# Three inverse channel stages drawn into the drain, the first two FFN parts split by group, and a new preparation plan

## The chip, the cores and the metric

The kernel runs on one core of one Trainium2 chip. The metric is the device time of one execution in microseconds. A kernel's executions agree within about 0.3%, so medians are given, and the figure that decides between two kernels is a ratio with a 95% interval. All times quoted are of fast runs; the mean granted TensorE clock from 46 to 150 us is 1.00 in the trace of every kernel here.

## The reference

A spectral filter with a residual, then an FFN with a squared ReLU and a residual:

```python
def reference(A_x, A_w_r, A_w_i, B_x, B_w1, B_b1, B_w2, B_b2):   # A_x: 1 x 2048 x 512, bf16; B_x is not read
    def A(x):                       # 2-D FFT, times a complex weight, inverse FFT
        X = rfft2(x) * (A_w_r + 1j * A_w_i)
        return irfft2(X, (2048, 512)).astype(bfloat16)
    def B(x):                       # FFN 512 -> 1792 -> 512
        h = relu(x @ B_w1 + B_b1)
        return (h * h) @ B_w2 + B_b2
    h = A_x + A(layernorm(A_x))
    return h + B(layernorm(h))
```

## The kernel before

The FFT is done with matmuls. Its last step, the inverse along the 512 channels, is done for one group of 128 rows at a time, in pieces that are placed among the FFN's matmuls: `s5` to `turn`. `PLAN[k]` says at which slot of chunk k-1 each piece of chunk k stands. A slot is one part of the FFN (14 up parts, then 4 down parts a group).

```python
def s5(g, ahead=False):                       # inverse channel stage of group g
    pe = bank("p5", "po", 2) if ahead else bank("p5", "pp", 3)
    for lt, tb, o in (...):                   # 4 small matmuls into one bank
        nc.tensor.matmul(pe[:, o:o + tb.shape[1]], lhsT=T2[...], rhs=tb, start=True, stop=True)
    def rest():
        nc.scalar.copy(V[...], pe[:])         # ACT takes the bank out
        nc.scalar.copy(H[:, :, 0:129:128], pe[...])
    if ahead: return rest
    rest()

def s5b(g):                                   # DVE: four operations with two SBUF inputs each
    H = V + V ; H = V - V ; R = H + H ; R = H - H
def s6(g):  matmul(py, lhsT=KI, rhs=R)        # PE
def s6a(g): hs[:, g] = py * WSC + xs[:, g]    # DVE, PSUM -> SBUF
# s6b statistics, rstd (ACT sqrt + DVE reciprocal), norm (DVE -> u),
# turn (transposes of u into UT: by PE for chunks 1 and 2, by DMA for chunks 3 and 4)

PLAN = {
    1: dict(s5=(-1, 1, 4), s5b=(-1, 1, 6), s6=(3, 7, 14), s6a=(3, 12, 14),
            s6b=(9, 14, 14), rstd=(15,), norm=(16, 16, 16), turn=(20, 20)),
    2: dict(s5=(1, 1, 3, 12), s5b=(1, 3, 11, 13), s6=(10, 10, 15, 16), s6a=(10, 10, 15, 16),
            s6b=(13, 16, 16, 16), rstd=(17,), norm=(17, 18, 20, 18), turn=(23, 24)),
    3: ..., 4: ...                            # see the diff
}
CHUNKS = ((0, 2), (2, 5), (5, 9), (9, 13), (13, 16))

def up(f):                                    # one up part of chunk c
    ph = bank("ph", "ph", 3)
    for d in range(ND):                       # 4 matmuls, n = 128 columns x groups of the chunk
        nc.tensor.matmul(ph[:, 0:n], lhsT=W1[:, d, bass.ts(f, P)], rhs=UT[:, d, 0:n], ...)
    nc.scalar.activation(rl, ph, ACT.Relu, ...)
    nc.vector.tensor_tensor(act[:, f], rl, rl, ALU.mult)
    # GpSimd's hb = hs + b2, needed by the output addition, tied to a square:
    mine = [a + f // 3] if c and f % 3 == 1 and f // 3 < b - a else range(a, b) if not c and f == NF - 1 else []
    for g in mine: nc.gpsimd.tensor_tensor(hb[:, g], hs[:, g], b2b, ALU.add)

def down(i, f0, f1):                          # po has two banks; ot = po + hb on DVE, then stored
    ...
    nc.vector.tensor_tensor(ot[:], po[:], hb[:, g, :], ALU.add)
    nc.sync.dma_start(ov[:, g, :], ot[:])     # the sync engine's queue, as the DMA transposes

# drain: groups 0 and 1 alone
rest = [s5(2, True), s5(3, True)]             # in the shadow of their LayerNorm
... LayerNorm, rest[0](), transposes of group 0, then of group 1 ...
s5b(2)
for c in range(5): run(c)
```

Of the kernel before, what the change touches and what calls it, by code (L numbers as in the profile page):

```python
# [15 lines left out]
P = 128  # L16
# [18 lines left out]
def kernel(  # L35
# [16 lines left out]
    nc = tc.nc  # L52
# [6 lines left out]
    ND = D // P  # L59
# [9 lines left out]
    W1 = persist.tile([P, ND, F], BF16, name="W1")  # L69
# [50 lines left out]
    def mm_tile(name, dt=FP32):  # L120
        return ps.tile([P, 4096 // mybir.dt.size(dt)], dt, tag="mm", name=name)
# [132 lines left out]
    def warm(o, n):  # L254

        for _ in range(n):
            nc.tensor.matmul(o, lhsT=ones[:, 0:P], rhs=ones[:], start=True, stop=True)  # L257
# [279 lines left out]
    def to_sqrt():  # L537
# [5 lines left out]
                  c=lambda k: butterfly(k, 1), A=lambda k: times_w(k, 0), B=lambda k: times_w(k, 1),  # L543
# [29 lines left out]
    def bank(name, tag, bufs, dt=FP32):  # L573
        return ps.tile([P, 2048 // mybir.dt.size(dt)], dt, tag=tag, name=name, bufs=bufs)

    Rs, Ys = {}, {}

    def s5(g, ahead=False):



        pe = bank("p5", "po", 2) if ahead else bank("p5", "pp", 3)
        for lt, tb, o in ((1, GI[:, 1, 0:129], 0), (3, GI[:, 3, 1:128], 129), (0, GI[:, 0, 0:128], 256),
                          (2, GIa[:, 1024:1152], 384)):
            nc.tensor.matmul(pe[:, o:o + tb.shape[1]], lhsT=T2[:, 2 * (lt % 2) + lt // 2, g].rearrange("p q s -> p (q s)"), rhs=tb,  # L585
                             start=True, stop=True)

        def rest():
            V = ffn.tile([P, 2, 2, 128], BF16, tag="V", bufs=3, name="V")
            H = ffn.tile([P, 2, 256], BF16, tag="H", bufs=3, name="H")  # L590
            nc.scalar.copy(V[:].rearrange("p e h c -> p (e h c)"), pe[:])  # L591
            nc.scalar.copy(H[:, :, 0:129:128], pe[:].rearrange("p (e h c) -> p e h c", e=2, h=2)[:, :, :, 0])
            Rs[g] = V, H

        if ahead:
            return rest
        rest()
# [67 lines left out]
    def transp(c, half):  # L665
# [11 lines left out]
        else:  # L677
# [1 line left out]


    PLAN = {
        1: dict(s5=(-1, 1, 4), s5b=(-1, 1, 6), s6=(3, 7, 14), s6a=(3, 12, 14),
                s6b=(9, 14, 14), rstd=(15,), norm=(16, 16, 16), turn=(20, 20)),
        2: dict(s5=(1, 1, 3, 12), s5b=(1, 3, 11, 13), s6=(10, 10, 15, 16), s6a=(10, 10, 15, 16),
                s6b=(13, 16, 16, 16), rstd=(17,), norm=(17, 18, 20, 18), turn=(23, 24)),
        3: dict(s5=(4, 5, 7, 15), s5b=(4, 8, 14, 15), s6=(10, 11, 18, 18), s6a=(11, 11, 18, 18),
                s6b=(13, 13, 20, 20), rstd=(16, 22), norm=(17, 17, 23, 23), turn=(19, 19, 23, 24)),
        4: dict(s5=(5, 5, 5), s5b=(5, 6, 7), s6=(10, 10, 14), s6a=(10, 15, 15),
                s6b=(14, 15, 17), rstd=(15, 22), norm=(18, 18, 22), turn=(19, 23, 22)),
    }  # L690

    def prep_steps(c):

        a = CHUNKS[c][0]
        n = CHUNKS[c][1] - a
        steps = []
        for kind, piece in (("s5", lambda k: rest[1]() if c == 1 and k == 1 else s5(a + k)), ("s5b", lambda k: s5b(a + k)),
                            ("s6", lambda k: s6(a + k)), ("s6a", lambda k: s6a(a + k)),
                            ("s6b", lambda k: s6b(a + k, on_act(c, a + k))),
                            ("rstd", lambda k: rstd(c, range(a + 2 * k, min(a + 2 * k + 2, a + n)) if c in BY_DMA else range(a, a + n))),  # L700
                            ("norm", lambda k: norm(c, a + k)), ("turn", lambda k: turn(c, k))):
            steps += [(slot, lambda piece=piece, k=k: piece(k)) for k, slot in enumerate(PLAN[c][kind]) if slot >= 0]
        return sorted(steps, key=lambda step: step[0])

    def mlp_slots(c):
        a, b = CHUNKS[c]
        n = P * (b - a)
        UT = UTs[c]
        act = ffn.tile([P, NF, 512], BF16, tag="act", bufs=2, name="act")
        slots = []  # L710

        def up(f):
            ph = bank("ph", "ph", 3)
            for d in range(ND):
                nc.tensor.matmul(ph[:, 0:n], lhsT=W1[:, d, bass.ts(f, P)], rhs=UT[:, d, 0:n],  # L715
                                 start=(d == 0), stop=(d == ND - 1))
            rl = ffn.tile([P, 512], BF16, tag="rl", bufs=6, name="rl")
            nc.scalar.activation(rl[:, 0:n], ph[:, 0:n], ACT.Relu, bias=b1f[:, f:f + 1], scale=1.0)  # L718
            sq = nc.vector.tensor_tensor(act[:, f, 0:n], rl[:, 0:n], rl[:, 0:n], ALU.mult)  # L719
            mine = [a + f // 3] if c and f % 3 == 1 and f // 3 < b - a else range(a, b) if not c and f == NF - 1 else []  # L720
            for g in mine:
                add = nc.gpsimd.tensor_tensor(hb[:, g, :], hs[:, g, :], b2b[:], ALU.add)  # L722
                tc.add_manual_dep(add.ins, sq.ins.name,
                                  mybir.DependencyInfo(mybir.DependencyClass.Sync, mybir.DependencyReason.DATA),
                                  reason="not before this square")

        state = {}

        def last(i):
            g = a + i  # L730
            ot = ffn.tile([P, D], BF16, tag="ot", bufs=3, name="ot")
            for h in range(2):
                po = bank("po", "po", 2)
                sl = slice(256 * h, 256 * h + 256)
                for f in range(NF):
                    nc.tensor.matmul(po[:, 0:256], lhsT=act[:, f, bass.ts(i, P)], rhs=W2[:, f, sl], start=(f == 0),  # L736
                                     stop=(f == NF - 1))
                nc.vector.tensor_tensor(ot[:, sl], po[:, 0:256], hb[:, g, sl], ALU.add)
                nc.sync.dma_start(ov[:, g, sl], ot[:, sl])

        def down(i, f0, f1):
            if c == 4 and i == b - a - 1:
                return last(i) if f0 == 0 else None
            if f0 == 0:
                state[i] = bank("po", "po", 2)
            po = state[i]
            for f in range(f0, f1):
                nc.tensor.matmul(po[:], lhsT=act[:, f, bass.ts(i, P)], rhs=W2[:, f, :], start=(f == 0), stop=(f == NF - 1))  # L748
            if f1 == NF:
                g = a + i  # L750
                ot = ffn.tile([P, D], BF16, tag="ot", bufs=3, name="ot")
                nc.vector.tensor_tensor(ot[:], po[:], hb[:, g, :], ALU.add)  # L752
                nc.sync.dma_start(ov[:, g, :], ot[:])

        for f in range(NF):
            slots.append(lambda f=f: up(f))
        for i in range(b - a):
            for f0, f1 in ((0, 4), (4, 8), (8, 11), (11, NF)):
                slots.append(lambda i=i, f0=f0, f1=f1: down(i, f0, f1))
        return slots  # L760
# [31 lines left out]
    for g in range(2):  # L792
        py = mm_tile("p6")[:, 0:512]
        if g == 0:
            nc.tensor.matmul(py, lhsT=identW[:], rhs=xs[:, 0, :], start=True, stop=False)
        for h in range(2):
            nc.tensor.matmul(py[:, 256 * h:256 * h + 256], lhsT=KI[:], rhs=R2[g][:, 256 * h:256 * h + 256],
                             start=(g == 1), stop=(g == 1 or h == 1))
        if g == 0:
            nc.scalar.activation(hs[:, 0, :], py, ACT.Copy, scale=WSC, accum_out=mv2[:, 0, 0:1])  # L800
        else:
            nc.vector.scalar_tensor_tensor(hs[:, 1, :], py, WSC, xs[:, 1, :], ALU.mult, ALU.add)
    warm(mm_tile("idle")[:, 0:512], 3)
    ps.release()
    ps = ctx.enter_context(tc.tile_pool(name="ps2", bufs=3, space=bass.MemoryType.PSUM))
    rest = [s5(2, True), s5(3, True)]
    idle = bank("idle", "ph", 3)
    s6b(0, True)
    st1 = ffn.tile([P, 6], FP32, tag="st", bufs=4, name="st2")
    nc.vector.bn_stats(st1[:], hs[:, 1, :])  # L810
    warm(idle[:], 4)
    nc.scalar.activation(sd2[:, 0:1], mv2[:, 0, 1:2], ACT.Sqrt, bias=eps[:], scale=float(D) ** -3)
    nc.vector.tensor_scalar(mv2[:, 0, 0:1], mv2[:, 0, 0:1], 1.0 / D, None, ALU.mult)
    nc.vector.reciprocal(rs2[:, 0:1], sd2[:, 0:1])
# [7 lines left out]
    for g, cp in ((0, nc.scalar.copy), (1, nc.vector.tensor_copy)):  # L822
        pt = bank("p7", "pp", 3, BF16)
        for d in range(ND):
            nc.tensor.transpose(pt[:, P * d:P * d + P], u2[:, g, bass.ts(d, P)], ident[:])
        cp(UTs[0][:, :, P * g:P * g + P], pt[:, 0:ND * P].rearrange("p (d c) -> p d c", d=ND))  # L826
    s5b(2)
    for c in range(5):
        run(c)
# [31 lines left out]
```

## Time and profile before

The time is 163.62 us (median; 163.61 to 163.63), the span in the profile 161.9. From 52.22 us on nearly everything is PE. A useful table is therefore where the first up matmul of each chunk stands on PE: the difference of two starts is the length of a stage, whatever else happens in it.

| first up matmul of | chunk 0 | chunk 1 | chunk 2 | chunk 3 | chunk 4 |
|---|---|---|---|---|---|
| before, us | 52.22 | 65.99 | 87.70 | 114.26 | 139.75 |
| length of that stage | 13.77 | 21.71 | 26.56 | 25.49 | to the end |

The timeline of PE (columns: start, duration from the first start to the modelled last end, operation, count, and in brackets idle time and what ended it) shows the waits of chunk 1 before:

```profile
76.45 1.89 PE L748 MATMUL po<-W,act 128*128 128x512 bf16 x8
78.43 0.38 PE L612 MATMUL p<-R,KI 128*128 128x512 bf16 x1
78.65 0.81 PE L748 MATMUL po<-W,act 128*128 128x512 bf16 x3
79.91 0.38 PE L612 MATMUL p<-R,KI 128*128 128x512 bf16 x1 [0.45 <-DVE R L608]
```

One matmul of 512 columns lasts 0.38 us, but the next starts 0.216 us after it has started (its pitch). The Trainium skill, "TensorE: Matmul & The Clock Gate", "Single matmul latency", gives (398 + N)/2.4 ns, which is 0.379 for N = 512: this is the duration the trace shows, and it holds 0.16 us in which the next matmul could already run.

### The profile page before, as it was taken

How to read it: one execution, taken by the hardware profiler on the slowest of the kernel's cores; microseconds unless marked ns; L12 is line 12 of the kernel's file. 1: busy time of each engine (PE TensorE's matmuls, PEld its weight loads, DVE VectorE, ACT ScalarE, POOL GpSimd, SP SyncE). 2: the span in 40 equal slices, each digit the busy share in tenths (PEclk: the TensorE clock that was granted, in tenths of full speed). 3: DMA queues.
4: the chain of work that ended last, by engine and by line, in shares of the span. 5: the costliest groups of instructions: out<-in, count | busy, mean ns of one | idle time of the engine just before them, and what ended most of it. 6: DMA issues, size and time to landing. Idle time of an engine off the chain costs nothing.

```text
span 161.9 us, 2721 instructions
## 1 busy us (share of the span) xinstructions
PE 151.0 (93%) x947; PEld 87.6 (54%) x947; DVE 124.7 (77%) x320; ACT 105.7 (65%) x203; POOL 37.9 (23%) x64
## 2 busy tenths in 40 slices
PE   2969899999997999999899999999999999999990
PEld 1447675878863874665345454434454444565470
DVE  6999899999947898699994589995379974287221
ACT  4999979999976970698543896731489760288000
POOL 7868750000200005035000244000052300052000
PEclk9999999999999999999999999999999999999998
DMA  4989299999000000200000100025200004200011
GB/s 143 364 249 138 44 204 203 362 369 187 11 0 0 4 0 2 71 0 0 0 32 32 36 0 0 2 65 117 82 0 2 0 20 110 69 32 0 6 59 34
DMA packets 16430, 12.34 MB, mean 76 GB/s; under 512 B 10784, under 2 KB 14880, under 8 KB 16416
## 3 DMA queue, kind: packets, MB, share of 16 engines
q1 hardware_dynamic: 16256, 11.25, 25.5%
q0 software_dynamic: 160, 0.92, 2.7%
q8 instruction: 7, 0.11, 0.3%
q14 instruction: 7, 0.06, 0.1%
HBM read 8.01 MB, written 2.10 MB: 62 GB/s over the span
## 4 chain that ended last, share of the span: by engine, by line
PE 76%; DVE 13%; ACT 4%; issue 2%; POOL 1%; ACTq 0%; DVEq 0%; POOLq 0%
PE po L748 27%; PE ph L715 25%; PE p L346 4%; DVE act L719 3%; DVE st L217 3%; PE p L500 2%; PE po L736 2%; PE p L612 2%; ACT rl L718 1%; PE p L585 1%; PE p L502 1%; PE p L503 1%; PE p L243 1%; DVE KFr L228 1%; PE p L672 1%
## 5 line engine op out<-in xcount | busy, mean ns | idle before, releaser
L718 ACT ACTIVATE rl<-ph,b1f 128x384 bf16<-128x384 f32 (+2 forms) x70 | 41.2, 616 | 22.6 <-PE ph L715 20.9
L715 PE MATMUL ph<-UT,W 128*128 128x384 bf16 (+2 forms) x280 | 51.6, 336 | 0.6 <-DVE UT L826 0.6
L748 PE MATMUL po<-W,act 128*128 128x512 bf16 x210 | 47.6, 379 | 0.0
L722 POOL TENSOR_TENSOR hb<-hs,b2b 128x512 f32<-128x512 bf16 x16 | 18.8, 1179 | 85.5 <-DVE act L719 85.5
L719 DVE TENSOR_TENSOR act<-rl 128x384 bf16<-128x384 bf16 (+2 forms) x70 | 31.3, 483 | 9.3 <-ACT rl L718 9.1
L715 PEld LDWEIGHTS <-W 128*128 128x128 bf16 x280 | 26.9, 98 | 21.1 <-issue 1.3
L748 PEld LDWEIGHTS <-act 128*128 128x128 bf16 x210 | 20.3, 98 | 24.8 <-issue 1.7
L752 DVE TENSOR_TENSOR ot<-po,hb 128x512 bf16<-128x512 f32 x15 | 10.3, 688 | 12.7 <-PE po L748 11.1
L257 PE MATMUL p<-ones 128*128 128x512 bf16 x23 | 7.5, 480 | 2.8 <-POOL ones L153 2.8
L616 DVE SCALAR_TENSOR_TENSOR hs<-p,xs 128x512 bf16<-128x512 f32 x14 | 9.1, 680 | 0.0
L243 PE MATMUL p<-KFr,xs 128*128 128x256 bf16 x32 | 7.3, 272 | 1.9 <-DVE KFr L228 1.9
L591 ACT CAST V<-p 128x512 bf16<-128x512 f32 x14 | 8.1, 593 | 0.0
L217 DVE BATCH_NORM_STATS2 st<-xs 128x6 f32<-128x512 bf16 x12 | 7.9, 676 | 0.0
L245 PE MATMUL p<-KFr,xs 128*128 128x256 bf16 x32 | 7.3, 272 | 0.0
L627 ACT ACTIVATE junk<-hs 128x512 bf16<-128x512 bf16 x6 | 3.8, 628 | 5.1 <-DVE hs L616 5.1
L257 PEld LDWEIGHTS <-ones 128*128 128x128 bf16 x32 | 3.5, 113 | 6.5 <-POOL ones L153 2.8
L508 ACT CAST T<-p 128x1024 bf16<-128x1024 f32 x7 | 6.9, 1039 | 0.1
L346 PE MATMUL p<-GF,Bt 128*128 128x256 bf16 x56 | 6.9, 273 | 0.0
L463 DVE TENSOR_TENSOR Z<-mA,mB 128x512 bf16<-128x512 bf16 x16 | 6.5, 420 | 0.1
L383 ACT CAST U<-p 128x1024 bf16<-128x1024 f32 x6 | 6.1, 1042 | 0.0
L252 ACT CAST Bt<-p 128x1024 bf16<-128x1024 f32 x6 | 5.9, 1010 | 0.3 <-PE p L245 0.3
L642 ACT ACTIVATE sd<-mv,eps 128x1 f32<-128x1 f32 (+2 forms) x10 | 2.7, 294 | 5.0 <-DVE mv L631 4.8
(188 smaller groups left out, 227.0 us busy)
## 6 DMA issues: line engine op xcount, KB each, us to landing
W<-in_B_w_dram SPq DMA_DIRECT2D x2, 1792.0 KB, 10.2
out_dram<-ot SPq DMA_DIRECT2D x15, 128.0 KB, 1.8
xs<-in_A_x_dram SPq DMA_DIRECT2D x3, 512.0 KB, 5.6
WB<-in_A_w_r_dram SPq DMA_DIRECT2D x1, 578.2 KB, 7.0
WB<-in_A_w_i_dram SPq DMA_DIRECT2D x1, 578.2 KB, 8.2
xs<-in_A_x_dram SPq DMA_DIRECT2D x2, 256.0 KB, 3.5
b2b<-in_B_b_dram SPq DMA_DIRECT2D x1, 128.0 KB, 9.5
out_dram<-ot SPq DMA_DIRECT2D x2, 64.0 KB, 1.5
```

What stands on the lines that cost most here:

```text
L217: nc.vector.bn_stats(st[:], xs[:, g, :])
L243: nc.tensor.matmul(o, lhsT=xs[:, g, P * t:P * t + P], rhs=KFr[:, g, 0:P].unsqueeze(1).to_broadcast([P, 2, P]), start=True, stop=False)
L257: nc.tensor.matmul(o, lhsT=ones[:, 0:P], rhs=ones[:], start=True, stop=True)
L346: nc.tensor.matmul(puv[:, :, e, :], lhsT=Bt[:, 2 * t + 1 - e, 2 * pr + q, :], rhs=GFv[:, t, :, e, :], start=(t == 0), stop=(t == 1))
L591: nc.scalar.copy(V[:].rearrange("p e h c -> p (e h c)"), pe[:])
L616: nc.vector.scalar_tensor_tensor(hs[:, g, :], Ys.pop(g)[:], WSC, xs[:, g, :], ALU.mult, ALU.add)
L715: nc.tensor.matmul(ph[:, 0:n], lhsT=W1[:, d, bass.ts(f, P)], rhs=UT[:, d, 0:n], start=(d == 0), stop=(d == ND - 1))
L718: nc.scalar.activation(rl[:, 0:n], ph[:, 0:n], ACT.Relu, bias=b1f[:, f:f + 1], scale=1.0)
L719: sq = nc.vector.tensor_tensor(act[:, f, 0:n], rl[:, 0:n], rl[:, 0:n], ALU.mult)
L722: add = nc.gpsimd.tensor_tensor(hb[:, g, :], hs[:, g, :], b2b[:], ALU.add)
L748: nc.tensor.matmul(po[:], lhsT=act[:, f, bass.ts(i, P)], rhs=W2[:, f, :], start=(f == 0), stop=(f == NF - 1))
L752: nc.vector.tensor_tensor(ot[:], po[:], hb[:, g, :], ALU.add)
```

## The change

The intent: get the inverse channel stages of groups 2 to 4 done while PE waits in the drain (group 2 before the hs of groups 0 and 1, with its copies on DVE; 3 and 4 after it, where 2 and 3 stood before), start the FFN as soon as the rows of group 0 are there by doing its first two up parts group by group, and choose new slots for all later preparation.

```diff
-    def s5(g, ahead=False):
-        pe = bank("p5", "po", 2) if ahead else bank("p5", "pp", 3)
+    def s5(g, pe=None, ahead=False):
+        if pe is None:
+            pe = bank("p5", "pp", 3)[:]
...
-        def rest():
+        def rest(cp=nc.scalar.copy):          # V and H copied by cp
...
     PLAN = {
-        1: dict(s5=(-1, 1, 4), s5b=(-1, 1, 6), s6=(3, 7, 14), s6a=(3, 12, 14),
-                s6b=(9, 14, 14), rstd=(15,), norm=(16, 16, 16), turn=(20, 20)),
-        2: dict(s5=(1, 1, 3, 12), s5b=(1, 3, 11, 13), s6=(10, 10, 15, 16), s6a=(10, 10, 15, 16),
-                s6b=(13, 16, 16, 16), rstd=(17,), norm=(17, 18, 20, 18), turn=(23, 24)),
-        3: dict(s5=(4, 5, 7, 15), s5b=(4, 8, 14, 15), s6=(10, 11, 18, 18), s6a=(11, 11, 18, 18),
-                s6b=(13, 13, 20, 20), rstd=(16, 22), norm=(17, 17, 23, 23), turn=(19, 19, 23, 24)),
-        4: dict(s5=(5, 5, 5), s5b=(5, 6, 7), s6=(10, 10, 14), s6a=(10, 15, 15),
-                s6b=(14, 15, 17), rstd=(15, 22), norm=(18, 18, 22), turn=(19, 23, 22)),
+        1: dict(s5=(-1, -1, -1), s5b=(-1, 0, 0), s6=(2, 5, 11), s6a=(3, 9, 14),
+                s6b=(10, 11, 14), rstd=(14,), norm=(16, 15, 16), turn=(20, 20)),
+        2: dict(s5=(1, 2, 6, 7), s5b=(2, 6, 7, 8), s6=(6, 11, 11, 14), s6a=(9, 11, 15, 16),
+                s6b=(14, 15, 18, 18), rstd=(18,), norm=(20, 20, 18, 18), turn=(22, 23)),
+        3: dict(s5=(0, 3, 5, 6), s5b=(1, 4, 6, 11), s6=(6, 7, 11, 15), s6a=(7, 8, 12, 15),
+                s6b=(10, 14, 17, 19), rstd=(16, 20), norm=(16, 17, 21, 22), turn=(16, 19, 21, 24)),
+        4: dict(s5=(0, 1, 1), s5b=(1, 3, 4), s6=(6, 6, 13), s6a=(7, 7, 13),
+                s6b=(11, 14, 14), rstd=(15, 14), norm=(17, 15, 17), turn=(18, 23, 24)),
     }
...
         def up(f):
+            if c == 0 and f == 0:             # parts 0 and 1, group 0 first, then group 1
+                first.update((k, bank("ph", "ph", 3)) for k in range(2))
+                for i in range(2):
+                    for k in range(2):
+                        for d in range(ND):
+                            nc.tensor.matmul(first[k][:, P * i:P * i + P], lhsT=W1[:, d, bass.ts(k, P)],
+                                             rhs=UT[:, d, P * i:P * i + P], ...)
...
         if g == 0:
+            s5(2, mm_tile("p5")[:, 0:512], True)(nc.vector.tensor_copy)
...
-    warm(mm_tile("idle")[:, 0:512], 3)
+    warm(mm_tile("idle")[:, 0:512], 2)
...
-    rest = [s5(2, True), s5(3, True)]
+    rest = [s5(3, None, True), s5(4, bank("p5", "po", 2)[:], True)]
...
-    warm(idle[:], 4)
+    warm(idle[:], 3)
...
+    rest[1]()
     s5b(2)
```

More of the change, by code (lines that the diff above doesn't have):

```diff
@@ L586, in s5 @@
                              start=True, stop=True)
-        def rest():
+        def rest(cp=nc.scalar.copy):
             V = ffn.tile([P, 2, 2, 128], BF16, tag="V", bufs=3, name="V")
             H = ffn.tile([P, 2, 256], BF16, tag="H", bufs=3, name="H")
-            nc.scalar.copy(V[:].rearrange("p e h c -> p (e h c)"), pe[:])
-            nc.scalar.copy(H[:, :, 0:129:128], pe[:].rearrange("p (e h c) -> p e h c", e=2, h=2)[:, :, :, 0])
+            cp(V[:].rearrange("p e h c -> p (e h c)"), pe)
+            cp(H[:, :, 0:129:128], pe.rearrange("p (e h c) -> p e h c", e=2, h=2)[:, :, :, 0])
             Rs[g] = V, H
@@ L696, in prep_steps @@
         steps = []
-        for kind, piece in (("s5", lambda k: rest[1]() if c == 1 and k == 1 else s5(a + k)), ("s5b", lambda k: s5b(a + k)),
+        for kind, piece in (("s5", lambda k: s5(a + k)), ("s5b", lambda k: s5b(a + k)),
                             ("s6", lambda k: s6(a + k)), ("s6a", lambda k: s6a(a + k)),
@@ L710, in mlp_slots @@
         slots = []
+        first = {}
         def up(f):
-            ph = bank("ph", "ph", 3)
-            for d in range(ND):
-                nc.tensor.matmul(ph[:, 0:n], lhsT=W1[:, d, bass.ts(f, P)], rhs=UT[:, d, 0:n],
-                                 start=(d == 0), stop=(d == ND - 1))
+            if c == 0 and f == 0:
[4 more added lines that the diff above has]
+                            nc.tensor.matmul(first[k][:, P * i:P * i + P], lhsT=W1[:, d, bass.ts(k, P)],
+                                             rhs=UT[:, d, P * i:P * i + P], start=(d == 0), stop=(d == ND - 1))
+            if f in first:
+                ph = first.pop(f)
+            else:
+                ph = bank("ph", "ph", 3)
+                for d in range(ND):
+                    nc.tensor.matmul(ph[:, 0:n], lhsT=W1[:, d, bass.ts(f, P)], rhs=UT[:, d, 0:n],
+                                     start=(d == 0), stop=(d == ND - 1))
             rl = ffn.tile([P, 512], BF16, tag="rl", bufs=6, name="rl")
```

## The prediction

> **Words used.** The 2048 rows are 16 groups of 128; the FFN takes them in five chunks: groups 0-1, 2-4, 5-8, 9-12, 13-15. A chunk is a row of slots: 14 "up" slots (4 matmuls and a ReLU each), then 4 "down" slots a group. Between the slots the next chunk is prepared: s5 (inverse channel stage: 4 small matmuls, then copies V and H), s5b (four DVE additions that make R), s6 (one matmul that reads R), s6a (hs = s6 + x), statistics, norm, transposes. The "drain" is the stretch after the last forward copies in which groups 0 and 1 go through alone.
>
> **What bounds the kernel now.** First the page's chain that ended last: matmuls of the FFN (L748 down, L715 up) hold half of the span.
>
> ```profile
> PE 76%; DVE 13%; ACT 4%; issue 2%; POOL 1%; ACTq 0%; DVEq 0%; POOLq 0%
> ```
>
> Then busy time by stage (columns: stretch, its length, busy time and count of PE, weight loads, DVE, ACT, POOL, granted clock, DMA).
>
> ```profile
> 46.00:52.22 6.22, 5.14 (x41) 3.03 (x42) 4.15 (x14) 4.33 (x12) 0.00 (x0) 1.00 0.00 0
> 52.22:66.09 13.87, 13.87 (x104) 9.47 (x105) 12.19 (x41) 7.86 (x20) 2.26 (x2) 1.00 0.01 2
> 66.09:87.86 21.77, 21.23 (x135) 11.73 (x134) 18.42 (x47) 14.22 (x33) 3.56 (x3) 1.00 0.08 25
> 87.86:114.34 26.48, 26.14 (x134) 12.09 (x132) 20.14 (x49) 15.34 (x34) 4.74 (x4) 1.00 0.16 39
> 114.34:139.92 25.58, 25.58 (x130) 11.96 (x129) 17.24 (x40) 14.69 (x31) 4.80 (x4) 1.00 0.14 38
> ```
>
> From 52.22 us on PE is saturated but for 0.54 us (chunk 1) and 0.34 us (chunk 2). PE's own waits name both, and the two of the drain:
>
> ```profile
> PE p L612 <- DVE R L608: 0.8, 2, 0.4
> PE ph L715 <- DVE UT L826: 0.6, 1, 0.6
> ```
>
> L612 is s6, waiting at 79.91 (0.45) and 105.77 (0.34) for R. L715 is the first up part, waiting for the transposed rows of group 1. So only three things can shorten the time: less matmul work after 52.22, an earlier first up part, fewer waits for R. The first part of the chain inside the drain shows what a later start there costs:
>
> ```profile
> 46.63 0.87 PE p5w L776 x8
> 47.50 0.21 PE p L795
> 47.72 0.30 PE p L797 x2
> 48.02 0.02 issue
> 48.04 0.70 ACT hs L800 x2
> ```
> ```profile
> 51.65 0.44 DVE UT L826
> 52.08 0.14 issue
> 52.22 1.91 PE ph L715 x16
> ```
>
> PE lies on this chain up to 48.02, then ACT and DVE do (LayerNorm of groups 0 and 1), then PE again.
>
> **What the Trainium skill says.** (1) "TensorE: Matmul & The Clock Gate", section "Wait — 56ns, not 53.3ns?": warm matmuls follow each other by N/2.4 GHz plus about 2.5 ns, so 128 columns cost half of 256. The trace agrees: 16 matmuls of 256 columns issue in 1.74 us (109 ns), 12 transposes of 128 take 0.67 (56 ns, each with its own weight load). Splitting a part by group is then nearly free. (2) Same page, "What's actually happening": the clock falls after an idle window of about 3.4 us. The change drops two filler matmuls; the longest PE idle of the drain is 0.61 us at clock 1.00, so I put nothing down for them. (3) "SBUF — State Buffer", "SBUF: two separate sides": a GpSimd operation and a DVE operation with two SBUF inputs exclude each other for the whole instruction. The trace agrees: beside this POOL addition one s5b addition takes 1.26 us, elsewhere 0.29.
>
> ```profile
> 68.60 1.15 POOL L722 TENSOR_TENSOR hb<-hs,b2b 128x512 f32<-128x512 bf16 x1 [5.44 <-DVE act L719]
> ```
> ```profile
> 68.64 1.26 DVE L603 TENSOR_TENSOR H<-V 128x254 bf16<-128x254 bf16 x1
> 71.16 0.29 DVE L603 TENSOR_TENSOR H<-V 128x254 bf16<-128x254 bf16 x1
> ```
>
> **The change, part by part.** The instruction order of the changed build gives the queues; durations are the trace's pitches.
>
> *1. s5 of group 2 into the drain.* It stands on PE between p5w (ends 47.50) and L795. Its bank is one that ACT has read by then, so it starts at once; 4 matmuls, 0.22-0.23 us (chain rows of L585), on the path: +0.22. Its copies go to DVE: V about as the other 128x512 PSUM copy there (692 ns, pitch near 0.6), H about 0.15, from about 47.8 to 48.6. DVE was idle 0.58 us there. hs of group 1 starts at 48.6 instead of 48.27 and its statistics end near 49.8; the DVE chain needs them only after the ACT square root, which moves from 49.91 to 50.13. So that is hidden. Sum +0.22.
>
> *2. s5 of groups 3 and 4 ahead.* Before, 2 and 3 stood in the drain's tail; now 3 and 4 do, in the shadow of the LayerNorm. Group 4's 4 matmuls leave the first chunk (they stood at 54.78): -0.22. ACT's V and H of group 4 (0.6 us) lie in ACT's idle 1.28 us ahead of the first ReLU.
>
> *3. First two up parts by group.* Rows of group 0 are copied by 51.63; with the same 0.14 us of issue PE can start at 51.78 instead of 52.22. Eight matmuls of 128 columns fill 0.44 us and end as group 1's rows arrive. The 16 matmuls cost what the 8 of 256 columns did (0.89 against 0.88). Gain 0.44.
>
> Sum of 1 to 3: +0.22 - 0.22 - 0.44 = **-0.44 us**.
>
> *4. The new plan.* Chunk 0: R of group 3 is ready near 54.5, s6 wants it at 54.8; no wait. Chunk 1, from T = its first up matmul (66.09 before): all four s5b now lie within slots 2 to 8. DVE's queue: act 1 ends T+2.43 as before. POOL's first addition holds act 2 until T+3.8; then s5b(5) 0.93, acts 3 and 4 (0.27 each) T+5.27; two acts and the second POOL hold (0.97 lost a time, from 72.64 to 73.87 against a pitch of 0.27) T+6.78; s5b(6) T+7.71; act 7 T+7.98; s5b(7) with the third hold T+9.88. PE reaches s6(7), now at slot 11, at 12 up parts x 0.65 + four s5 x 0.22 + two s6 x 0.22 = T+9.1. So it waits **about 0.8 us** there, where the kernel before waited 0.45 for R of group 8 (now ready long before its slot 14). The transposes now stand a slot earlier, and DVE's norms end near T+18.8 against PE's arrival at T+18.65: 0.1 more. Net of chunk 1: **+0.45**.
>
> Chunk 2: the s5b of groups 9 to 12 go forward to slots 1 to 11; the tightest is R(10), ready at T+7.95 for an s6 at T+8.0. The 0.34 us of before goes, with perhaps 0.1 in its place: **-0.25**. Chunk 3: the tightest is R(14), T+6.8 for T+6.95: 0. The last chunk and the final store are unchanged.
>
> Sum: -0.44 + 0.45 - 0.25 = -0.24 us, so near 163.4. The plan was evidently chosen anew by someone who could try many, so I lean a little lower than my ledger: **163.2 us**.
>
> **Rivals.** (a) *The plan removes the waits for R altogether*: R(7) comes in time because the POOL additions fall at kinder moments or PE reaches slot 11 later (ACT is near its limit in chunk 1: 14 ReLUs of 0.55 and four pairs of copies are 10 us beside PE's 9.1 us of up parts, so PE may lose small bits at the up parts instead). Then -0.44 - 0.79 = 162.4. For it: the whole plan moves s5b forward, which can only serve R. Against it: DVE was bound without a gap from 72.18 to 79.86 in the chain of before, and the new order adds a third s5b ahead of the s6 that wants it. (b) *DVE's backlog grows and is passed on*: s6(7) waits 1.2, the norms are late and the transposes wait 0.5 more: 164.0. For it: DVE is busy 18.42 of 21.77 us in this stage; against it: DVE's sum of work is unchanged, only its order. (c) *The drain loses more*: if DVE's copy of V delays hs of group 1 past the square root, up to 0.4 us is added and the gain of parts 1 to 3 is gone: 163.6. Against it: 0.2 us of slack after the 0.58 us gap.
>
> **Range and chances.** The rivals span 162.4 to 164.0; the repeat spread is 0.01 us (163.61 to 163.63). Two per cent is 3.3 us, more than all PE idle after 46 us (1.08 in the drain and 0.88 later) plus the moved matmuls, so a verdict of faster is all but impossible. Slower needs a new wait of more than 3 us, of which no queue shows a sign. Prediction 163.2, range 162.4 to 163.9; faster 0.02, within 0.97, slower 0.01.
>
> **What would show it right or wrong.** The first ReLU matmul of the FFN some 0.2 us earlier than 52.22, as 16 matmuls of 128 columns with no gap of 0.6 ahead of the second half; the hs activation of group 0 0.2 us later than 48.04; four fewer small s5 matmuls after 52; PE's wait for R at the s6 of group 7 in chunk 1 near 0.8 us, and none in chunk 2 above 0.1. If PE shows no wait for R at all, step 4 is wrong (rival a). If the ReLU of the first up part starts later than 52.9, steps 1 to 3 are. If waits of L715 for ACT appear in chunk 1, ACT has become the bound there, which I left out.

## More of the kernel before

The sync engine's queue near the end of chunk 3 has one row each for a DMA transpose of chunk 4 or an output store, in the order in which they were issued:

```profile
132.95 1.20 SPq L661 DMA_TRANSPOSE UT<-u  x1
134.69 0.33 SPq L753 DMA_DIRECT2D out_dram<-ot  x1
135.21 2.50 SPq L661 DMA_TRANSPOSE UT<-u  x2
```

And on DVE the first output addition of that chunk stands directly behind one reciprocal:

```profile
131.63 0.17 DVE L643 RECIPROCAL rs<-sd 128x2 f32<-128x2 f32 x1 [0.36 <-ACT sd L642]
131.74 0.69 DVE L752 TENSOR_TENSOR ot<-po,hb 128x512 bf16<-128x512 f32 x1
```

## The result, and the profile after

The changed kernel takes 163.93 us (163.91 to 163.95; 4 runs) against 163.62: ratio 1.0019, interval 1.0001 to 1.0036, so the same at 2% and probably a trifle slower. A ratio is the mean time of one kernel's fast runs over that of the other's of the same rounds, so not quite the ratio of the medians quoted. Executions over 1.5% slower than the fastest of the same kernel are left out of the means. The prediction was 163.2 with a range up to 163.9: the measurement lies 0.73 above it and 0.03 above the range.

The stages show where it went:

| stage (first up matmul to first up matmul) | before | after | difference |
|---|---|---|---|
| start to chunk 1 (drain and chunk 0) | 65.99 | 65.41 | -0.58 |
| chunk 1 | 21.71 | 22.30 | +0.59 |
| chunk 2 | 26.56 | 26.38 | -0.18 |
| chunk 3 | 25.49 | 25.83 | +0.34 |
| chunk 4 and store, to the end of the span | 22.12 | 22.20 | +0.08 |
| sum | | | +0.25 |

The spans of the two profiles (161.87 and 162.12 us in the packed traces) differ by this sum. The medians differ by 0.31: the profiled executions were not the median ones (163.66, 0.04 above, and 163.91, 0.02 below), which is the other 0.06. In the last stage the matmuls take as long as before (18.37 and 18.36 us); the 0.08 lies behind the last of them.

**The drain.** The timeline of PE at the start of the FFN, before and then after:

```profile
52.22 1.91 PE L715 MATMUL ph<-UT,W 128*128 128x256 bf16 x16 [0.61 <-DVE UT L826]
```
```profile
51.80 1.05 PE L721 MATMUL ph<-UT,W 128*128 128x128 bf16 x16
```

The 16 matmuls of 128 columns start 0.42 earlier and run without a gap: 1.05 - 0.16 = 0.89 us for 16, 56 ns each.

**Chunk 1.** PE after; the first two rows are the s6 of groups 6 and 7, the last is the first half of the transposes:

```profile
74.31 0.38 PE L613 MATMUL p<-R,KI 128*128 128x512 bf16 x1
75.52 0.39 PE L613 MATMUL p<-R,KI 128*128 128x512 bf16 x1 [0.82 <-DVE R L609]
...
78.12 6.21 PE L761 MATMUL po<-W,act 128*128 128x512 bf16 x28
84.38 0.89 PE L673 MATMUL p<-ident,u 128*128 128x128 bf16 x8
```

The s6 of group 7 could have followed that of group 6 at 74.31 + 0.22 = 74.53 and came at 75.52: 0.99 late, 0.82 of it shown. The 28 down matmuls are through by 78.12 + 28 x 0.2163 = 84.18, so the transposes start 0.20 late without any bracket, and 8 of them take 0.89 where 0.61 is the undisturbed figure (`a3_pool_late_c1` below): 0.28 more. In all 0.99 + 0.47 = 1.46 us, against 0.86 before. On DVE, which both wait for, and on GpSimd:

```profile
68.60 0.78 DVE L732 TENSOR_TENSOR act<-rl 128x384 bf16<-128x384 bf16 x1 [0.66 <-ACT rl L731]
...
73.67 1.26 DVE L605 TENSOR_TENSOR H<-V 128x254 bf16<-128x254 bf16 x1
...
75.18 0.28 DVE L609 TENSOR_TENSOR R<-H 128x256 bf16<-128x256 bf16 x1
...
83.26 1.38 DVE L654 TENSOR_SCALAR u<-hs,mv,rs 128x512 bf16<-128x512 bf16 x4
```
```profile
73.63 1.15 POOL L735 TENSOR_TENSOR hb<-hs,b2b 128x512 f32<-128x512 bf16 x1 [1.50 <-DVE act L732]
```

R(7) is the R of group 7. One addition on the way to it takes 1.26 beside the GpSimd addition of 73.63 to 74.78, the last one 0.28. The two GpSimd additions before (68.02 and 70.93) fall on squares: the one shown takes 0.78, another, at 71.22, 1.13, where an undisturbed one takes 0.35. The three hold DVE by 0.42, 0.78 and 0.98 us. R(7) is complete at 75.46 and PE starts the s6 at 75.52. The four norms run from 83.26 to 84.64; in the order of the plan, the groups that the transposes take first (5 and 6) are normed third and fourth.

**Chunk 3.** Three views of the kernel after, on DVE, on the weight loads of PE, and on the sync engine's queue:

```profile
132.07 0.16 DVE L644 RECIPROCAL rs<-sd 128x1 f32<-128x1 f32 x1 [1.14 <-ACT sd L643]
132.44 0.17 DVE L644 RECIPROCAL rs<-sd 128x2 f32<-128x2 f32 x1 [0.21 <-ACT sd L643]
132.64 0.41 DVE L654 TENSOR_SCALAR u<-hs,mv,rs 128x512 bf16<-128x512 bf16 x1
132.97 0.68 DVE L765 TENSOR_TENSOR ot<-po,hb 128x512 bf16<-128x512 f32 x1
```
```profile
133.71 5.71 PEld L761 LDWEIGHTS <-act 128*128 128x128 bf16 x27 [0.29 <-issue]
```
```profile
134.18 1.19 SPq L662 DMA_TRANSPOSE UT<-u  x1
135.47 0.53 SPq L766 DMA_DIRECT2D out_dram<-ot  x1
136.05 2.50 SPq L662 DMA_TRANSPOSE UT<-u  x2
```

The new plan puts both square roots, both reciprocals and a norm ahead of the first output addition. That addition ends at 133.65 instead of 132.43, and only then is its PSUM bank free for the third down group, which starts at 133.71 although PE could have begun at about 133.55: **0.17**. The store of that addition goes ahead of the first transpose in the queue. So the queue, in the same order as before, stands 0.8 to 1.2 us later (134.18 against 132.95, 136.05 against 135.21): the last transpose goes out at about 137.3, lands 2.4 us later (the page's median from issue to landing), and the first up part of chunk 4 begins at 139.92 instead of 139.75: **0.17** again. The page names no waiter for either: of a loss of 0.17 the tail hides 0.16 us.

In chunk 2 the 0.50 of before became 0.15 at the s6 of group 10 and 0.28 at the end, where the last DMA transpose goes out at about 111.4 and lands 2.4 us later, and the first up part of chunk 3 starts at 114.09. (The kernel before lost 0.03 and 0.06 more in two other places of that chunk; with them the gain is near the 0.18.)

### The profile page after: what moved, and what is told of

The parts are those of the page before. It is cut to its first block, busy times and chain, and to the rows that moved or that the text cites. A ratio compares the mean times of both kernels' runs of the same rounds, so it can differ in the third digit from the quotient of the medians.

```text
span 162.1 us, 2727 instructions
## 1 busy us (share of the span) xinstructions
PE 150.9 (93%) x953; PEld 87.2 (54%) x953; DVE 122.9 (76%) x322; ACT 105.0 (65%) x201; POOL 38.1 (23%) x64
## 4 chain that ended last, share of the span: by engine, by line
PE 72%; DVE 11%; ACT 9%; DMA 3%; issue 1%; POOL 1%; SPq 1%; ACTq 0%; DVEq 0%
PE ph L728 24%; PE po L761 24%; PE p L346 4%; DMA xs<-in_A_x_dram 3%; ACT junk L209 3%; DVE act L732 3%; PE p L500 2%; PE po L749 2%; DVE hs L617 2%; PE p L613 1%; ACT rl L731 1%; DVE H L605 1%; ACT Bt L252 1%; PE p L586 1%; PE p L503 1%
## 5 line engine op out<-in xcount | busy, mean ns | idle before, releaser
L728 PE MATMUL ph<-UT,W 128*128 128x512 bf16 (+2 forms) x272 | 51.2, 339 | 0.1
L761 PE MATMUL po<-W,act 128*128 128x512 bf16 x210 | 47.1, 380 | 0.0
L728 PEld LDWEIGHTS <-W 128*128 128x128 bf16 x272 | 26.0, 98 | 20.3 <-issue 1.3
L732 DVE TENSOR_TENSOR act<-rl 128x384 bf16<-128x384 bf16 (+2 forms) x70 | 27.6, 426 | 10.7 <-ACT rl L731 10.4
L605 DVE TENSOR_TENSOR H<-V 128x254 bf16<-128x254 bf16 x14 | 7.9, 565 | 0.0
L592 ACT CAST V<-p 128x512 bf16<-128x512 f32 x13 | 7.6, 588 | 0.0
```

The lines of the kernel that those rows point to most:

```text
L592: cp(V[:].rearrange("p e h c -> p (e h c)"), pe)
L605: nc.vector.tensor_tensor(H[:, :, 255:128:-1], V[:, :, 0, 1:128], V[:, :, 1, 1:128], ALU.subtract)
L732: sq = nc.vector.tensor_tensor(act[:, f, 0:n], rl[:, 0:n], rl[:, 0:n], ALU.mult)
L761: nc.tensor.matmul(po[:], lhsT=act[:, f, bass.ts(i, P)], rhs=W2[:, f, :], start=(f == 0), stop=(f == NF - 1))
```

## The experiments

All twelve kernels gave correct results. In the short diffs "after" is the changed kernel. Medians of 4 or 5 runs (3 fast ones for `c1_best`). None differs from the kernel before by 2%: what is read here are differences of some tenths in time that stand in the stages too.

**The new plan of chunk 1 taken back**, and with it those of chunks 2 and 3, leaving only the drain and chunk 0:

```diff
 a2_plan2_before: after, with
-    2: (new)
+    2: (old)
 a4_drain_only:   after, with
-    2, 3, 4: (new)
+    2, 3, 4: (old)
```

> Changed kernel with the old plan for chunk 1 alone (rows of chunk 2 prepared). Theory (the new plan of chunk 1 costs 0.59 us there: 22.30 us against 21.71 from first up part to first up part): chunk 1 back near 21.7 us, about 163.3 us, PE wait for R of 0.45 at the s6 of group 8 and 0.25 more at group 7. Rival (chunk 1 is bound by the sum of DVE's work, and an earlier start only waits longer): stage stays 22.3 us, no change.

> Changed kernel with the old plans for chunks 1, 2 and 3, so that only the drain, the split first up parts and the plan of chunk 0 are new. Theory (they gain 0.58 us by the first up part of chunk 1, and nothing takes it back): about 163.05 us. Rival (the gain is absorbed by fixed later arrivals, the DMA transposes of chunks 3 and 4): between 163.3 and 163.6 us.

Measured: `a2` 163.36 (ratio to before 0.9977, 0.9959 to 0.9995), `a4` 163.10 (0.9961, 0.9943 to 0.9979). Chunk 1 is 21.71 us again in both, to the hundredth. So the new plan of chunk 1 costs 0.57, and the three later plans together 0.83 (in the stages 0.59 - 0.18 + 0.34 + 0.08). The drain and the plan of chunk 0 alone give a kernel half a microsecond faster than before. Both came as the theory said.

**The other way round: only the three later plans, on the kernel before.**

```diff
 b1_plans_only: before, with
-    2, 3, 4: (old)
+    2, 3, 4: (new)
```

> Kernel before with the new plans for chunks 1, 2 and 3 and nothing else of the change. Theory (the plans cost 0.59 us in chunk 1, gain 0.18 in chunk 2, cost 0.34 in chunk 3, whatever comes ahead of them): 163.62 + 0.75, about 164.4 us. Rival (they hurt only in company of the new drain, which brings chunk 1's DVE work forward): 163.6 us or less.

Measured 164.49 (1.0047, 1.0029 to 1.0065): +0.87. The loss does not depend on the drain: chunk 1 takes 22.31 and chunk 3 25.83, as in the changed kernel.

**The drain in its parts.**

```diff
 b2_split_only: before, with only the first two up parts group by group
 d2_s5_only:    a4_drain_only, with the first two up parts as before
```

> Kernel before with the two first up parts split by group and nothing else of the change. Theory: 16 matmuls of 128 columns start at 51.8 instead of 52.22, gain 0.4 us, kept to the end since later stages of the kernel before have their waits tied to PE's own pace: about 163.2 us. Rival (DVE-bound waits for R stand at fixed times and swallow it): 163.6 us.

> Old plans for chunks 1 to 3, first up parts whole: of the change only s5 of groups 2 to 4 ahead and the plan of chunk 0. Theory (the parts add up: drain with split gained 0.56 in time, split alone 0.36): gain about 0.2 us, 163.45 us, the first up part at 52.3 to 52.4 (later than 52.22 by the 4 matmuls on the path), the first up part of chunk 1 about 0.2 us earlier than before. Rival (moving s5 gains nothing by itself, since it costs in the drain what it saves in chunk 0, and it helps only the split): 163.6 us.

Measured: `b2` 163.30 (0.9974, 0.9956 to 0.9991), `d2` 163.54 (0.9997, 0.9983 to 1.0011). The split alone starts at 51.68 and has its third part at 52.57 instead of 53.09, a gain of 0.52, but chunk 1 starts only 0.32 earlier: part of it is lost within chunk 0. The largest piece is 0.13 at the fourth up part, which starts at 53.13 and not at 53.00; presumably it waits for the first of the three `ph` banks, which ACT's ReLU of the first part, from 52.61 on, has to read. In `d2` the time decides nothing: the gain against the kernel before of the same rounds is 0.09, between the theory's 0.2 and the rival's 0, and the interval includes 1. The trace says more. The early s5 alone leave the FFN waiting for the rows of group 1, and those come later by what the s5 of group 2 cost:

```profile
52.35 0.82 PE L716 MATMUL ph<-UT,W 128*128 128x256 bf16 x6 [0.61 <-ACT H L593]
```

That is 0.13 after the 52.22 of before. (The bracket names an ACT copy that ended at 52.33, but these matmuls do not read H; DVE's copy of the rows of group 1 ends at 52.21, and PE follows 0.14 us later, as in the kernel before from 52.08 to 52.22.) Chunk 1 starts at 65.89, 0.10 earlier. Together (`a4`) the start of chunk 1 moves by 0.55, more than 0.32 + 0.10.

**What the loss of chunk 1 hangs on.** First the GpSimd additions of chunk 1 moved behind its last square, in the changed kernel:

```diff
 a3_pool_late_c1
-    mine = [a + f // 3] if c and f % 3 == 1 and ... else range(a, b) if not c and f == NF - 1 else []
+    mine = [a + f // 3] if c > 1 and f % 3 == 1 and ... else range(a, b) if c < 2 and f == NF - 1 else []
```

> Changed kernel, but the three GpSimd additions of chunk 1 stand after its last square, as those of chunk 0 do. Theory (each addition holds DVE for about 0.97 us ahead of R of group 7, 2.9 us in all): the 0.82 us wait for R goes, the wait of the transposes too, chunk 1 near 20.9 us instead of 22.3, about 162.5 us. Rival (GpSimd holds DVE just as long later, when the norms are due): the wait for R goes but the transposes wait as long; about 163.9 us.

Measured 162.47 (0.9922, 0.9905 to 0.9940): 1.46 us under the changed kernel, 1.15 under the one before. Chunk 1 takes 20.81, just what its matmuls fill: 56 x 0.1622 up, 42 x 0.2163 down, 16 x 0.0555 s5, 16 x 0.056 transposes and 4 x 0.2163 s6 are 20.82. PE shows both of the earlier waits gone:

```profile
74.42 0.59 PE L613 MATMUL p<-R,KI 128*128 128x512 bf16 x2
...
83.27 0.61 PE L673 MATMUL p<-ident,u 128*128 128x128 bf16 x8
```

So the wait for R(7) and the one for the norms are one thing: DVE's row, held by the three GpSimd additions (0.42, 0.78 and 0.98 us). In their new place, from 77.71 to 81.09, DVE does hs and output additions and statistics, with one SBUF input each, and these take 0.66 to 0.69 us as elsewhere.

Is the GpSimd placement alone worth that much? The same edit on the kernel before, with its old plan:

> Kernel before with only the GpSimd additions of chunk 1 after its last square. Theory (PE's waits for R in chunk 1 of the kernel before, 0.25 at group 7 and 0.61 at group 8 counted from the issue of the matmul before, come from the three holds of DVE too): both go, chunk 1 20.9 us for 21.71, about 162.8 us. Rival (in that plan s5b of groups 7 and 8 stand so late that R is late even without holds): 163.4 us or more.

A miss, and in the other direction: 164.43 (1.0042, 1.0025 to 1.0060). The wait at the s6 of group 7 does go, as the theory said. But in the old plan the s5b of group 8 stands at slot 13, just where the three additions now run in one row (78.00 to 81.65). DVE, and the waits of PE in the whole run (1.53 of it at the s6 of group 8; the other is the 0.34 of chunk 2):

```profile
78.36 1.12 DVE L607 TENSOR_TENSOR R<-H 128x256 bf16<-128x256 bf16 x1
79.41 1.23 DVE L608 TENSOR_TENSOR R<-H 128x256 bf16<-128x256 bf16 x1
```
```profile
PE p L612 <- DVE R L608: 1.9, 2, 1.5
```

The rival's number (163.4 or more) held, but not its cause: R is late by the holds, moved on to it. Of these two plans, the edit pays only in the one where all the s5b come before it. The new plan ends them at slot 8, and had thus made room that it did not use.

Then the wait attacked from its other end, by reading R later:

```diff
 b4_s6_turn_later: after, PLAN[2]
-    s6=(6, 11, 11, 14)   turn=(22, 23)
+    s6=(6, 11, 13, 14)   turn=(23, 24)
```

> Changed kernel; in chunk 1 the s6 of group 7 stands at slot 13 for 11 and the transposes at slots 23 and 24 for 22 and 23. Theory (DVE's sum of work bounds this chunk): the 0.82 us wait for R goes, PE then waits some 0.6 us for the norms at the transposes, chunk 1 near 21.4 us for 22.3, about 163.1 us. Rival (the wait for R is the whole cost, and no later one takes its place): chunk 1 near 20.9 us, 162.5 us as with the GpSimd additions moved.

Measured 163.20 (0.9967, 0.9949 to 0.9985); chunk 1 took 21.57, so 0.75 is still lost. The size fits the theory that a wait of DVE's queue is passed on, but the place does not: the transposes wait no more, and in their stead the s6 of group 8 waits for its PSUM bank, which an hs addition on DVE has to free:

```profile
PE p L613 <- DVE hs L617: 0.6, 1, 0.6
```

**What the loss of chunk 3 hangs on.** First only the slots of the transposes, and so the order of the queue, then DVE's order as well:

```diff
 a1_turns_together: after, PLAN[4]
-    turn=(18, 23, 24)
+    turn=(18, 19, 19)
 b5_store_first: after, PLAN[4]
-    rstd=(15, 14), norm=(17, 15, 17), turn=(18, 23, 24)
+    rstd=(17, 17), norm=(17, 17, 17), turn=(18, 19, 19)
```

> Changed kernel, but the three DMA transposes of the last chunk stand together (slots 18, 19, 19 for 18, 23, 24), ahead of the store of the second output group in the sync engine's queue. Theory (the last chunk's first up part waits for a late transpose: PE leaves 0.34 us free at 139.58 to 139.92): the gap closes, transposes are issued some 0.6 us earlier, about 163.6 us. Rival (PE waits for something else there, or the profile's gap is only its modelled ends): no change, 163.93.

> Changed kernel; in the last chunk's preparation the square roots, reciprocals, norms and transposes all stand at slots 17 to 19 (from 14 to 24), so that DVE's first output addition of chunk 3 goes ahead of the reciprocals and the transposes ahead of the second store. Theory (chunk 3 loses 0.17 us because the third down group waits for the accumulator that the late first output addition frees, and 0.17 us because the last transpose lands late): both go, 163.6 us, the first up part of chunk 4 at 139.6. Rival (only the transposes matter): as the run with the transposes together, 163.7 us, and the 0.17 us at 133.5 stays.

Measured: `a1` 163.68 (0.9994, 0.9977 to 1.0012), `b5` 163.46 (0.9984, 0.9966 to 1.0001). As the theories said, in `a1` the transposes go out in one row, ahead of the second store, and the wait before chunk 4 is gone, but the gap ahead of the third down group stays. Its queue and its weight loads:

```profile
134.24 3.81 SPq L662 DMA_TRANSPOSE UT<-u  x3
```
```profile
133.76 0.53 PEld L761 LDWEIGHTS <-act 128*128 128x128 bf16 x3 [0.29 <-issue]
```

In `b5` the first output addition comes before the square roots are asked for, and both are gone: chunk 3 takes 25.49, what it took before the change. The 0.08 at the very end has gone in both runs too (from the first up matmul of chunk 4 to the end 22.12 in `a1`, 22.08 in `b5`).

```profile
130.88 0.69 DVE L765 TENSOR_TENSOR ot<-po,hb 128x512 bf16<-128x512 f32 x1
```

**All together, and once more.**

```diff
 c1_best:  a3_pool_late_c1, PLAN[4] of b5, and PLAN[3]
+    s6=(6, 8, 11, 15), s6a=(7, 9, 12, 15), s6b=(10, 14, 14, 16),
+    rstd=(16, 17), norm=(16, 17, 18, 18), turn=(16, 18, 18, 19)
 d1_best2: c1_best, PLAN[3]
+    s6b=(10, 12, 15, 16), rstd=(13, 17), norm=(14, 14, 18, 18), turn=(14, 15, 18, 19)
```

> All findings together: the changed kernel, the GpSimd additions of chunk 1 after its last square, the last chunk's preparation as in the run with the store first, and in chunk 2 the s6 of group 10 a slot later and its norms and transposes forward. Theory (the gains are additive where they remove PE's gaps: 1.46 us in chunk 1, 0.34 to 0.47 in chunk 3, 0.15 for R of group 10 and 0.28 for the late transposes of chunk 2): 163.93 - 2.2 to 2.3, about 161.7 us, 1.2% under the kernel before. Rival (with PE faster, the transposes through the sync engine or DVE become the bound in chunks 2 and 3): 162.2 us, gaps before the first up parts of chunks 3 and 4.

> As the run with all findings, but in chunk 2 the norms and DMA transposes of groups 9 and 10 go at slots 14 and 15, ahead of those of 11 and 12 (before, all but one stood in a row after slot 17, and PE waited 0.49 us for the last). Theory (a row of transposes costs 1.25 us of the sync engine's queue each plus 2.4 us to land; two of them out of the way bring the last one in by 111 us, PE arrives at 112.4): the 0.49 us goes, about 161.8 us. Rival (the norms of groups 9 and 10 at that place delay DVE's other work for PE, so another wait takes its place): 162.2 us.

Measured: `c1` 162.26 (0.9910, 0.9888 to 0.9931), `d1` 162.20 (0.9916, 0.9903 to 0.9930). Both beat both kernels by about 0.8 to 1.1%, and in both the rival's number won: half a microsecond waits somewhere else in chunk 2, which takes 26.66 and 26.60. (The gap before chunk 4 that the rival of `c1` also named did not come: chunk 3 takes 25.49.) In `c1` the transposes of chunk 3 went out too close to its start, in `d1` the earlier statistics pushed a square of chunk 2 behind them. The waits of PE, `c1` and then `d1`:

```profile
PE ph L728 <- DMA UT<-u: 0.5, 1, 0.5
```
```profile
PE po L761 <- DVE act L732: 0.5, 1, 0.5
```

## Why the prediction was wrong

| step of the prediction | predicted | measured |
|---|---|---|
| 1 to 3, drain and first parts | -0.44 | -0.58 |
| 4, chunk 1 | +0.45 | +0.59 |
| 4, chunk 2 | -0.25 | -0.18 |
| 4, chunk 3 | 0 | +0.34 |
| 4, last chunk and store | 0 | +0.08 |
| leaning lower than the ledger | -0.18 | 0 |

With the 0.06 by which the profiled executions lie off the medians, the last column comes to +0.31; the middle one comes to -0.42.

**Steps 1 to 3 were right in mechanism; their sizes were not.** Step 3 puts the first up part at 51.78, but step 1 adds 0.22 ahead of it: the ledger, and the sign "some 0.2 us earlier than 52.22", mean 52.0. It stands at 51.80. s5 of group 2 moves the hs of group 0 by 0.13 (48.04 to 48.17) and not by 0.22, presumably since the KI matmuls had waited about 0.08 for R before (the four took 0.68, now 0.60); and PE follows the copy of the rows of group 0, which ends at 51.74, after 0.06 where 0.14 was put down. Chunk 0 in turn got shorter by 0.16 (13.61 for 13.77) and not by the 0.22 of step 2. The splitting is free, as said. The early s5 and the split need each other, as `b2` and `d2` show: the sum of steps treated them as independent, and that happened to be on the safe side.

**Step 4, chunk 1, was right in mechanism and cause.** R(7) was put at T + 9.88 and came at 75.46 - 65.41 = T + 10.05; PE's arrival was put at T + 9.1 and came at T + 9.12. The trace shows a wait of 0.82 where 0.8 was forecast, but these are not counted alike: the forecast counts from PE's arrival, and from there the s6 was 0.99 late. The net was off by 0.14 because three errors nearly cancel. The wait cost 0.99 for 0.8. The transposes were put at 0.1 and cost 0.47: the same backlog of DVE reaches the norms. And what the kernel before lost was taken from its waits, 0.45, when by the starts it was 0.86. That the net came so near is luck. `a3` shows the cause by taking it away: without the GpSimd additions in that stretch, 1.49 us of chunk 1 go.

**Step 4, chunk 3, failed.** "Chunk 3: the tightest is R(14), T+6.8 for T+6.95: 0." R(14) was indeed no matter, but the step looked at R alone and left out what else stands in DVE's and the sync engine's rows. This is the step that failed: 0 was forecast, and 0.34 was measured. The plan of chunk 4 also moved square roots, norms and transposes: the reciprocals now hold up DVE's first output addition, thus a PSUM bank, and, by the store of that addition, the transposes behind it in a queue that sends them one by one. `a1` and `b5` take the two apart: 0.17 each in the profile. Not tested is whether DVE's order alone, with the transposes left in their slots, would have cured both. The same omission shows in chunk 2, where 0.28 is lost at the late transposes that no step names, and in "the last chunk and the final store are unchanged", which cost 0.08.

**The leaning failed.** The plan was taken for one that someone had found by trying, and 0.18 was subtracted for it. Nothing in the profile supported that. `b1` shows the three later plans to cost 0.87 whatever the drain does, and `a4` shows that without them the change is worth 0.5 us, near what steps 1 to 3 said. Rival (b), "DVE's backlog grows and is passed on", described what happened, transposes included, at 164.0 us: it was held for too unlikely, though the ledger already contained its first half. That its total also comes near the 163.93 is luck: it knew nothing of the 0.34 and 0.08 of chunk 3 and the end.

What stays open is how the 0.08 us behind the last matmul comes about. It goes with the plan of chunk 4: from its first up matmul to the end of the span, the five traces with that plan as changed have 22.19 or 22.20 us (the changed kernel, `a2`, `a3`, `b1`, `b4`), the nine others 22.08 to 22.12. Moving the transposes alone (`a1`) takes it away, so `a1`'s 0.25 us is 0.17 of chunk 3 and this 0.08; but no trace was found to name the wait.

## What to carry to other kernels

Measure a stage by the starts of the matmuls against the sum of their pitches, not by the idle time shown: in these traces the tail of a 512-column matmul hides 0.16 us of every wait behind it, and it hid half of what one stage lost. When work is moved forward on a shared engine, follow each thing that stands behind it in its queue, including the bank that its output frees and the DMA queue that it feeds, not only the wait that it is to serve. And look for what holds the engine: the GpSimd additions, in no bottleneck themselves, cost more than everything the change gained (1.49 us against 0.58), and moving them paid only once the operations that they hold had been cleared out of their new place.

## What the Trainium skill lacked or had wrong

- "TensorE: Matmul & The Clock Gate", "Back-to-back issue gap", gives for a stream in which each matmul has its own weight load about 81 ns at N = 128 and 131 ns at N = 512. The traces here show 56 ns (16 matmuls with 16 weight loads in 0.89 us) and 216 ns (28 down matmuls with their loads in 6.06 us), which are the figures that the same page calls isolated.
- The same page, "Single matmul latency", fits the durations (0.38 us at N = 512), but neither it nor "Perfetto Trace Analysis" was found to say that a wait shorter than duration less pitch, 0.16 us, leaves no idle time in the profile, and that longer ones appear shorter by as much: 0.61 us was shown as 0.45.
- "DMA: Bandwidth & Descriptors", "DMA Transpose (X-bar)", has constraints but no time; elsewhere the page has a bandwidth, and sequencer cycles for a transpose of 8,192 tiles, but nothing for one as small as here. One of 128x512 bf16 from SBUF to SBUF holds the issuing queue 1.2 to 1.27 us (3.81 for three), and 2.4 us pass from issue to landing.
- "SBUF — State Buffer", "SBUF: two separate sides", is right on the exclusive lock, and the runs put a price on it: three GpSimd additions of 1.15 to 1.20 us held DVE by 0.42, 0.78 and 0.98 us, and moving them out of the way took 1.49 us off that stage.
